# A fused attention and two-stage expert kernel: the first 256 tokens go through attention by themselves, and the first two tiles of the first layer are computed for each half of the first block

## The chip, the core and the metric

The kernel runs on one core of a Trainium2 chip. A core has a matrix engine (TensorE, PE in the rows; its weight loads are PEld), a vector engine (VectorE, DVE), a scalar engine (ScalarE, ACT), a general engine (GpSimd, POOL) and a queue engine (SyncE, SP), from which most transfers are issued. Each engine works through its own list of instructions in order and waits for the others by semaphores. The metric is the device time of one execution in microseconds (us), the median of several runs.

## What is computed

The reference has three stages, one behind the other, over 3072 tokens of width 512:

```python
for t in range(S):                                   # attention with a decaying state, 4 batches x 8 heads, S = 768
    state = gamma * state + outer(k[t], v[t])
    y[t] = scale * q[t] @ state
x = y.transpose(0, 2, 1, 3).reshape(3072, 512)
x = ((x @ w_a) * (x @ w_b)) @ w_out                  # first layer, d_ff 1536
e = argmax(x @ w_gate)                               # second layer: one of 8 experts for each token
out = gate * sigmoid_of_e * (relu(x @ w1[e]) @ w2[e])
```

The first layer's weights come as 64-bit numbers, and the kernel narrows them to pairs of 32-bit numbers (a high and a low part) on the chip.

## The kernel before

**Blocks.** The tokens are cut into seven blocks (BLOCKS, five of 512 tokens and two of 256). For each block the first layer runs over 12 tiles of 128 of its 1536 columns, counted by f. Tile f has two projections (`proj`, one bank p0 for w_a and one p1 for w_b, each 12 matmuls of 512 columns: 4 pieces of the model width, 3 matmuls each for high and low parts), then `act_a` (ScalarE copies p0 to a_sb), `gate` (VectorE multiplies p1 by a_sb into g_sb, L540; ScalarE casts g_sb to the high part of gs, L542; VectorE subtracts for the low part, L543), and one tile later `down` (12 matmuls that add gs times w_out into the banks acc0 to acc3). The banks p0 and p1 exist once: the second projection of tile f+1 can't start before the multiplication of tile f has read p1.

**Attention.** It goes by batches, two for every 256 tokens (one for each half of the heads). Batch n has `prep_q` and `prep_v` (decayed copies qd and vd, on VectorE or GpSimd), `scores` (matmuls L181 and L185 into two sc banks, VectorE masks them into m, L189, and adds up the states, L192; GpSimd decays the last state, L195) and `outputs` (matmuls L205 and L211 into two y banks, ScalarE copies, L217, VectorE adds, L220). For block 0 the result goes through a tile z straight into xs (high part by ScalarE, L223, low part by VectorE, L224); for the others it goes to xraw. While block j is in the first layer, the attention of block j+1 is run in slots between its projections (`attention_steps`, `steps`).

**Narrowing.** The weights arrive as 36 tiles of 512 KB, in the order of their use: w_a and w_b of f = 0, w_out of 0, w_a and w_b of 1, and then for each f the two projections of f + 2 and w_out of f + 1. Four buffers (wide) hold them raw. For each tile ScalarE makes e_cv (L441) and r_cv (L446), VectorE joins them in two operations on whole 128x512 tiles (L487, L489) into w_cv, ScalarE casts w_cv into the high part (L457), and GpSimd subtracts for the low part (L458); that lands in arena (w_a, w_b) or wos (w_out). The list of these steps is a generator, and `narrow(k)` takes the next k steps of it, four for each tile, two of them ending at one VectorE operation each. So the place of the narrow calls in the program fixes where these operations stand in each engine's list. In the first layer of block 0 there are 12 steps, three tiles, for each f: narrow(4) behind the first projection, behind the gate and behind down.

**The start.** `keep_warm` runs matmuls whose result isn't used. Then come the four attention batches of block 0 (batches 0 and 1 are the first 256 tokens, 2 and 3 the second), as steps of scores and outputs: scores 0, scores 1, outputs 0, scores 2, outputs 1, scores 3, outputs 2, outputs 3, with narrow(3) behind each from the third on. Only then does the first projection start, on all 512 tokens of block 0.

Of the kernel before, what the change touches and what calls it, by code (L numbers as in the profile page):

```python
# [7 lines left out]
F32 = mybir.dt.float32  # L8
# [35 lines left out]

NARROW_FROM, CONST_AT = 2, 5

# [7 lines left out]
def attention_moe_moe2(ctx: ExitStack, tc: tile.TileContext, a: dict, out: bass.AP):  # L54
# [54 lines left out]
    def f32(ap):  # L109
        return ap.bitcast(F32)  # L110
# [86 lines left out]
    def outputs(n, xr, toff):  # L197
# [14 lines left out]
        if xr is None:  # L212
            z, cols = p2.tile([128, 2, 256], F32, tag="gs", name="z"), slice(0, 256)
        else:
            z, cols = xr[:, 2 * pp : 2 * pp + 2], slice(toff, toff + 256)
# [12 lines left out]
    def prep_all(n):  # L228
        prep_q(n)
        prep_v(n)  # L230

    def attention_steps(j):
        own = [(ci, 2 * c + pp) for ci, c in enumerate(BLOCKS[j]) for pp in range(2)]

        def put(ci, n):
            if j == 0:
                xraw[j] = None
            elif j not in xraw:
                xraw[j] = p1.tile([128, KD, 512], F32, tag="xraw", name="xraw")
            outputs(n, xraw[j], 256 * ci)  # L240

        def s_a(n):
            scores(n)
            m = {0: 3, 1: 4, 2: None}.get(n, n + 2)
            if m and m < len(batches):
                load_batch(m)

        def s_b(ci, n, nxt):
            put(ci, n)
            if nxt is not None:  # L250
                prep_all(nxt)

        steps = []
        if j == 0:

            for i, (ci, n) in enumerate(own):
                steps.append(lambda n=n: s_a(n))
                if i:
                    steps.append(lambda p=own[i - 1], nxt=n + 1: s_b(*p, nxt if nxt <= len(own) else None))
            steps.append(lambda: s_b(*own[-1], None))  # L260
        else:
            for i, (ci, n) in enumerate(own):

                nxt = n + 1 if n + 1 < len(batches) and not (j == 1 and i + 1 == len(own)) else None
                steps.append(lambda n=n: s_a(n))
                steps.append(lambda ci=ci, n=n, nxt=nxt: s_b(ci, n, nxt))
        return steps
# [234 lines left out]
    def narrow(k):  # L502
        for _ in range(k):
            next(narrowing, None)
# [18 lines left out]

    def proj(j, f, ab, n):
        p = ps1.tile([128, 512], F32, tag=f"p{ab}", name=f"p{ab}")
        for k in range(KD):
            kk = slice(128 * k, 128 * k + 128)
            mm3(p[:, :n], arena[:, f, ab, 0, kk], arena[:, f, ab, 1, kk], xs[:, 0, k, :n], xs[:, 1, k, :n], k == 0, k == KD - 1)
        return p
# [7 lines left out]

    def gate(j, f, ta, pb, n):
        g = p1.tile([128, 512], F32, tag="g_sb", name="g_sb")
        dve.tensor_tensor(g[:, :n], pb[:, :n], ta[:, :n], op=ALU.mult)  # L540
        gs = p2.tile([128, 2, 512], F32R, tag="gs", name="gs")
        act.copy(gs[:, 0, :n], g[:, :n])  # L542
        dve.tensor_tensor(gs[:, 1, :n], g[:, :n], f32(gs[:, 0, :n]), op=ALU.subtract)  # L543
        gt[j, f] = gs

    accs = {}

    def down(j, f, ntile):
        gs, w = gt.pop((j, f)), wos.pop((j, f))
        for t in range(ntile):  # L550
# [226 lines left out]
    with tc.manual_schedule():  # L777
# [16 lines left out]
        load_batch(1)  # L794
        next_wide()
        load_batch(2)
        next_wide()
        next_wide()
        next_wide()
        tri_f = p1.tile([128, 2, 128], F32, tag="g_sb", name="tri_f")  # L800

        prep_all(0)
        prep_all(1)
        for n, st in enumerate(attention_steps(0)):
            st()
            keep_warm(WARM_STEP)
            if n >= NARROW_FROM:
                narrow(3)
            if n == CONST_AT:
                sync.dma_start(tri_f, a["tri"])  # L810
                sync.dma_start(base8, a["base8"])
                sync.dma_start(ident, a["ident"])
                sync.dma_start(wg, a["wg"])
                sync.dma_start(iota8, a["iota8"])
                sync.dma_start(pay, a["pay"])
                sync.dma_start(tab_d[:, :], a["tab0"])
        dve.tensor_copy(tri, tri_f)
        dve.tensor_copy(ohsum, base8)
        spare.clear()

        tok0 = 0
        route = []
        for j, blk in enumerate(BLOCKS):
# [4 lines left out]
            if last:  # L828
# [3 lines left out]
                route += [lambda: turn((0, 0), xs, LEAD), lambda: turn((0, 1), xs, LEAD + 128)]  # L832
            nslots = 3 * NF1 - 3
            lines = [att, route]
# [18 lines left out]

            for f in range(NF1):
                if f + 2 < NF1:
# [25 lines left out]
                if f > 0:  # L881
                    down(j, f - 1, ntile)
                if j == 0:
# [3 lines left out]
                if f == NF1 - 1:  # L887
                    down(j, f, ntile)
                slot()
# [115 lines left out]
```

## Time and profile before

| what | value |
|---|---|
| median of 3 runs | 1039.01 us (1038.29 to 1041.26) |
| the profiled execution, its own time | 1041.96 us |
| its span from first to last instruction | 1040.1 us |
| mean granted TensorE clock | 0.986 |
| first projection of block 0 starts | 37.27 us |
| first projection of block 1 starts | 155.95 us |

Between these two starts lies the first layer of block 0, with the narrowing of all weights and the attention of block 1. The profiled execution took 2.95 us more than the median of the runs, and 1.86 us of its own time lie outside its span. Places in the text are microseconds from the span's start.

### The profile page before, as it was taken

What the parts mean: (1) busy time and instruction counts of PE and PEld (TensorE: products, weight loads), DVE (VectorE), ACT (ScalarE), POOL (GpSimd) and SP (SyncE); (2) the same over time, 40 slices, a digit from 0 to 9 for tenths busy, and PEclk for the clock granted to TensorE, in tenths of its full rate; (3) what the DMA queues carried; (4) which work ended last, traced back from release to release, by engine and by line L of the source; (5) the groups of instructions that cost most, each with busy time, mean ns of one, the idle gap of its engine ahead of it and who ended that gap; (6) DMA issues with size and microseconds to landing.
All of it is one profiled execution on the core that took longest, in us unless ns stands there. A gap on an engine that the chain in (4) does not pass through costs nothing. (4 is left out here: it accounts for less than half of the span.)

```text
span 1040.1 us, 19789 instructions
## 1 busy us (share of the span) xinstructions
PE 1008.6 (97%) x7701; PEld 845.2 (81%) x7702; DVE 610.4 (59%) x1383; ACT 383.9 (37%) x775; POOL 278.9 (27%) x241
## 2 busy tenths in 40 slices
PE   6899999999999999999999999999999999999997
PEld 4687778887888788878888888999898978789996
DVE  5799886755577547755775484463365544345531
ACT  2466662222322332223222323553354434344431
POOL 1455541114111411132212333341322020221211
PEclk7799999999999999999999999999999999999999
DMA  8676635322433242234122422450564442435510
GB/s 326 205 236 215 224 122 176 129 82 53 154 110 101 84 153 98 85 94 159 55 91 62 127 88 71 132 183 21 182 203 156 157 155 102 155 134 167 190 67 28
DMA packets 51676, 138.63 MB, mean 133 GB/s; under 512 B 10973, under 2 KB 11229, under 8 KB 51552
## 3 DMA queue, kind: packets, MB, share of 16 engines
q1 hardware_dynamic: 43920, 117.16, 33.8%
q0 software_dynamic: 6928, 19.46, 5.9%
q8 instruction: 69, 1.13, 0.4%
q10 hardware_dynamic: 720, 0.57, 0.2%
q14 instruction: 39, 0.32, 0.1%
HBM read 121.37 MB, written 16.96 MB: 133 GB/s over the span
## 5 line engine op out<-in xcount | busy, mean ns | idle before, releaser
L105 PE MATMUL p<-xs,arena 128*128 128x512 f32 (+1 forms) x672 | 248.4, 370 | 8.7 <-DVE g_sb L540 4.5
L107 PE MATMUL p<-xs,arena 128*128 128x512 f32 (+1 forms) x672 | 242.4, 361 | 0.5 <-POOL arena L458 0.5
L106 PE MATMUL p<-xs,arena 128*128 128x512 f32 (+1 forms) x672 | 242.6, 361 | 0.0
L515 POOL TENSOR_TENSOR wos<-wo,wos 128x512 fp32r<-128x512 f32 x72 | 99.1, 1377 | 283.4 <-ACT wos L514 280.6
L105 PEld LDWEIGHTS p<-xs,arena 128*128 128x128 f32 x672 | 127.2, 189 | 32.4 <-issue 9.5
L107 PEld LDWEIGHTS p<-xs,arena 128*128 128x128 f32 x672 | 127.4, 190 | 20.7 <-POOL arena L458 1.0
L106 PEld LDWEIGHTS p<-xs,arena 128*128 128x128 f32 x672 | 127.4, 190 | 18.8
L542 ACT CAST gs<-g_sb 128x512 fp32r<-128x512 f32 (+1 forms) x84 | 47.0, 559 | 214.4 <-DVE g_sb L540 212.9
L340 DVE SCALAR_TENSOR_TENSOR junkd<-x,wcol 128x512 bf16<-128x512 f32 x144 | 121.1, 841 | 5.2 <-DMA wcol<-in_wgt 1.6
L105 PE MATMUL acc<-wos,gs 128*128 128x512 f32 x288 | 115.2, 400 | 0.0
L107 PE MATMUL acc<-wos,gs 128*128 128x512 f32 x288 | 113.2, 393 | 0.0
L106 PE MATMUL acc<-wos,gs 128*128 128x512 f32 x288 | 112.7, 391 | 0.0
L637 DVE SCALAR_TENSOR_TENSOR hs<-ph,hs 128x384 fp32r<-128x384 f32 (+2 forms) x72 | 40.1, 558 | 121.9 <-ACT hs L636 108.9
L671 DVE TENSOR_TENSOR arena<-wraw,arena 128x512 fp32r<-128x512 f32 x112 | 76.5, 692 | 48.4 <-ACT arena L670 38.6
L540 DVE TENSOR_TENSOR g_sb<-p,a_sb 128x512 f32<-128x512 f32 (+1 forms) x84 | 51.3, 611 | 79.2 <-PE p L107 70.1
L657 POOL DMA_INDIRECT out<-y,idx x27 | 27.9, 1032 | 237.2 <-ACT y L656 155.5
L105 PE MATMUL acc<-arena,hs 128*128 128x512 f32 x216 | 86.7, 402 | 2.1 <-ACT hs L636 1.5
L670 ACT CAST arena<-wraw 128x512 fp32r<-128x512 f32 x112 | 67.9, 616 | 49.7 <-PE acc L107 35.6
L107 PE MATMUL acc<-arena,hs 128*128 128x512 f32 x216 | 85.8, 397 | 0.0
L106 PE MATMUL acc<-arena,hs 128*128 128x512 f32 x216 | 85.4, 395 | 0.0
L636 ACT ACTIVATE hs<-ph 128x384 fp32r<-128x384 f32 (+2 forms) x72 | 35.4, 491 | 134.4 <-PE ph L107 88.9
L543 DVE TENSOR_TENSOR gs<-g_sb,gs 128x512 fp32r<-128x512 f32 (+1 forms) x84 | 52.3, 623 | 52.5 <-ACT gs L542 51.2
(147 smaller groups left out, 1698.8 us busy)
## 6 DMA issues: line engine op xcount, KB each, us to landing
wraw<-in_ex SPq DMA_DIRECT2D x64, 512.0 KB
wo<-wo_d SPq DMA_DIRECT2D x72, 256.0 KB
wide<-in_w_ab SPq DMA_DIRECT2D x24, 512.0 KB
qk<-in_qk SPq DMA_DIRECT2D x23, 512.0 KB
vk<-in_vk SPq DMA_DIRECT2D x23, 512.0 KB
wcol<-in_wgt SPq DMA_DIRECT2D x20, 512.0 KB
wide<-in_w_out SPq DMA_DIRECT2D x12, 512.0 KB
x_d<-x SPq DMA_DIRECT2D x24, 256.0 KB
```

Source lines behind the costliest of these rows:

```text
L105: pe.matmul(outp, lhsT=wh, rhs=rh, start=start, stop=False)
L106: pe.matmul(outp, lhsT=wh, rhs=rl, start=False, stop=False)
L107: pe.matmul(outp, lhsT=wl, rhs=rh, start=False, stop=stop)
L340: dve.scalar_tensor_tensor(junk, x2t[i], 1.0, wc[:, e], op0=ALU.mult, op1=ALU.mult, accum_out=st["lg"][:, e0 + e : e0 + e + 1])
L515: pool.tensor_tensor(w[:, 1], t, f32(w[:, 0]), op=ALU.subtract)
L540: dve.tensor_tensor(g[:, :n], pb[:, :n], ta[:, :n], op=ALU.mult)
L542: act.copy(gs[:, 0, :n], g[:, :n])
L543: dve.tensor_tensor(gs[:, 1, :n], g[:, :n], f32(gs[:, 0, :n]), op=ALU.subtract)
L636: act.activation(h[:, 0, :n], p[:, :n], AF.Relu)
L637: dve.scalar_tensor_tensor(h[:, 1, :n], p[:, :n], 0.0, f32(h[:, 0, :n]), op0=ALU.max, op1=ALU.subtract)
L670: act.copy(arena[:, f, part, 0], t[:, part])
L671: dve.tensor_tensor(arena[:, f, part, 1], t[:, part], f32(arena[:, f, part, 0]), op=ALU.subtract)
```

## The change

The 256 tokens of batches 0 and 1 are scored and finished first: scores 0, scores 1, outputs 0, outputs 1, with narrow steps between. Then comes scores 2, and then the first two tiles (f = 0 and 1, HALVES = 2) are computed on columns 0 to 255 of block 0 (`chunk(f, 0, ...)`), while scores 3, outputs 2 and outputs 3 stand between their projections; then `down` for the first two token tiles, and the same two tiles on columns 256 to 511. The loop over f starts at 2 for block 0, and the attention of block 1 starts there too: its 8 steps are spread over the 10 tiles that are left. A chunk is one half of a tile's two projections, with narrow(4) behind each; there are 16 narrow steps before the first chunk and 54 before f = 2. Before the change there were 18 before f = 0 and 42 before f = 2. The tile z takes its buffers from the ring of w_cv, the constant tri_f from that of wo, and the transfers of the constants move to the end of this part. The second layer and all later blocks are the same.

```diff
-NARROW_FROM, CONST_AT = 2, 5
+HALVES = 2
...
         if xr is None:
-            z, cols = p2.tile([128, 2, 256], F32, tag="gs", name="z"), slice(0, 256)
+            z, cols = e5.tile([128, 512], F32, tag="w_cv", name="z").rearrange("p (k n) -> p k n", k=2), slice(0, 256)
...
-    def proj(j, f, ab, n):
+    def proj(j, f, ab, n, c0=0):
...
-            mm3(p[:, :n], arena[:, f, ab, 0, kk], arena[:, f, ab, 1, kk], xs[:, 0, k, :n], xs[:, 1, k, :n], k == 0, k == KD - 1)
+            mm3(p[:, :n], arena[:, f, ab, 0, kk], arena[:, f, ab, 1, kk], xs[:, 0, k, c0 : c0 + n], xs[:, 1, k, c0 : c0 + n], k == 0, k == KD - 1)
...
-        for n, st in enumerate(attention_steps(0)):
-            st()
-            keep_warm(WARM_STEP)
-            if n >= NARROW_FROM:
-                narrow(3)
...
+        scores(0)
+        load_batch(3)
+        keep_warm(WARM_STEP)
+        narrow(2)
+        scores(1)
+        keep_warm(WARM_STEP)
+        narrow(4)
+        outputs(0, None, 0)
+        prep_all(2)
+        keep_warm(WARM_STEP)
+        outputs(1, None, 0)
+        prep_all(3)
+        narrow(6)
+        keep_warm(WARM_STEP)
+
+        spare[:] = ["acc2", "acc3"]
+        scores(2)
+        narrow(4)
+        rest = [lambda: (scores(3), load_batch(4)), lambda: (outputs(2, None, 256), prep_all(4)), lambda: outputs(3, None, 256), lambda: spare.clear()]
+
+        def chunk(f, c0, beside):
+            pa = proj(0, f, 0, 256, c0)
+            ta = act_a(pa, 256)
+            beside()
+            narrow(4)
+            pb = proj(0, f, 1, 256, c0)
+            gate(0, f, ta, pb, 256, c0)
+            beside()
+            narrow(4)
...
+        for f in range(HALVES):
+            chunk(f, 0, beside)
...
+        down(0, 0, 0, 2)
+        narrow(2)
+        for f in range(HALVES):
+            chunk(f, 256, lambda: None)
+            if f + 1 < HALVES or HALVES == 1:
+                down(0, f, 2 if f == 0 else 0, 4)
+            narrow(2)
...
-            nslots = 3 * NF1 - 3
+            f0 = 0 if j else HALVES
+            nslots = 3 * (NF1 - f0) - 3
...
-            for f in range(NF1):
+            for f in range(f0, NF1):
```

TensorE, ahead of the first projection (p_618 and p_452 are its bank p0, sc and y the banks of scores and outputs). Before, behind the outputs of batch 3:

```order
L205 MATMUL y<-qd,state 64x64 x16
L211 MATMUL y<-m,vd 64x64 x16
L783 LDWEIGHTS tri
L783 MATMUL wp<-tri 128x256
L105 MATMUL p_618<-xs,arena 128x512
L106 MATMUL p_618<-xs,arena 128x512
L107 MATMUL p_618<-xs,arena 128x512
```

Now, behind the scores of batch 2:

```order
L181 MATMUL sc<-qd,stage 64x64 x8
L185 MATMUL sc<-vd,stage 64x64 x8
L105 MATMUL p_452<-xs,arena 128x256
L106 MATMUL p_452<-xs,arena 128x256
L107 MATMUL p_452<-xs,arena 128x256
```

The first projection moved ahead of scores 3, outputs 2 and outputs 3, and it has half the columns.

VectorE, from the gate of tile 0 to that of tile 1. Before (g_sb_698 is tile 0, g_sb_807 tile 1):

```order
L540 TENSOR_TENSOR g_sb_698<-p1_685,a_sb_631 128x512
L543 TENSOR_TENSOR gs_700<-g_sb_698,gs_700 128x512
L489 SCALAR_TENSOR_TENSOR w_cv_642<-wide_430,w_cv_642 128x512
L487 SCALAR_TENSOR_TENSOR w_cv_712<-e_cv_640,r_cv_706 128x512
L489 SCALAR_TENSOR_TENSOR w_cv_712<-wide_492,w_cv_712 128x512
L487 SCALAR_TENSOR_TENSOR w_cv_723<-e_cv_710,r_cv_717 128x512
L489 SCALAR_TENSOR_TENSOR w_cv_723<-wide_559,w_cv_723 128x512
L487 SCALAR_TENSOR_TENSOR w_cv_749<-e_cv_721,r_cv_743 128x512
L220 TENSOR_TENSOR xraw_751<-xraw_751,y_752 128x2x2x64
L220 TENSOR_TENSOR xraw_751<-xraw_751,y_753 128x2x2x64
L540 TENSOR_TENSOR g_sb_807<-p1_794,a_sb_738 128x512
```

Now, for the second halves (g_sb_750 is tile 0, g_sb_821 tile 1):

```order
L529 TENSOR_TENSOR g_sb_750<-p1_737,a_sb_722 128x256
L534 TENSOR_TENSOR gs_540<-g_sb_750,gs_540 128x256
L478 SCALAR_TENSOR_TENSOR w_cv_735<-wide_593,w_cv_735 128x512
L476 SCALAR_TENSOR_TENSOR w_cv_763<-e_cv_733,r_cv_757 128x512
L478 SCALAR_TENSOR_TENSOR w_cv_763<-wide_660,w_cv_763 128x512
L476 SCALAR_TENSOR_TENSOR w_cv_797<-e_cv_761,r_cv_776 128x512
L478 SCALAR_TENSOR_TENSOR w_cv_797<-wide_689,w_cv_797 128x512
L529 TENSOR_TENSOR g_sb_821<-p1_808,a_sb_793 128x256
```

Almost as many joining operations (L476, L478, which were L487, L489) now stand between two gates of half a tile as stood between two of a whole one. In VectorE's whole list 17 of the 72 stood ahead of the last gate shown before, and 24 stand ahead of the last one shown now. Five more stand between that and the gate of tile 2, and six between two gates from there on, as before; so ahead of the gate of tile 9 there are 71 now, which is the number that stood ahead of the gate of tile 10.

GpSimd, around the preparation of batch 4 (qd_546 and vd_548 before, qd_584 and vd_586 now; the low part of w_b of tile 1, which is the fifth weight tile, is made from w_cv_614 before and from w_cv_516 now). Before:

```order
L458 TENSOR_TENSOR arena_84<-w_cv_378,arena_84 128x512
L139 TENSOR_TENSOR qd_546<-qk_259,dec_88 128x512
L146 TENSOR_TENSOR vd_548<-vk_260,vtab_89 128x512
L458 TENSOR_TENSOR wos_609<-w_cv_438,wos_609 128x512
L458 TENSOR_TENSOR arena_84<-w_cv_556,arena_84 128x512
L458 TENSOR_TENSOR arena_84<-w_cv_614,arena_84 128x512
```

Now:

```order
L195 TENSOR_TENSOR state_86<-state_86,gc_90 128x128
L447 TENSOR_TENSOR arena_84<-w_cv_441,arena_84 128x512
L139 TENSOR_TENSOR qd_584<-qk_510,dec_88 128x512
L146 TENSOR_TENSOR vd_586<-vk_511,vtab_89 128x512
L447 TENSOR_TENSOR arena_84<-w_cv_516,arena_84 128x512
```

The low parts of the third and fourth weight tile now stand ahead of batch 4, and that of the fifth stands right behind it. On SP the two transfers of batch 4 now stand behind the refills of all four wide buffers; before, they stood ahead of the first refill.

## Rows read from the trace of the kernel before

**Rows 1.** The page: busy time by engine, and TensorE's clock in 40 slices.

```profile
PE 1008.6 (97%) x7701; PEld 845.2 (81%) x7702; DVE 610.4 (59%) x1383; ACT 383.9 (37%) x775; POOL 278.9 (27%) x241
PEclk7799999999999999999999999999999999999999
```

**Rows 2.** Timeline of TensorE: start, duration, instruction, [idle before <- what ended it].

```profile
32.66 0.50 PE L783 MATMUL wp<-tri 128*128 128x256 bf16 x3
37.27 0.77 PE L105 MATMUL p<-xs,arena 128*128 128x512 f32 x1 [4.11 <-DVE z L220]
...
42.41 0.46 PE L181 MATMUL sc<-qd,qk 64*64 64x64 f32 x16
...
43.50 0.50 PE L105 MATMUL p<-xs,arena 128*128 128x512 f32 x1
...
49.20 0.69 PE L205 MATMUL y<-qd,state 64*64 64x64 f32 x32
...
50.30 0.50 PE L105 MATMUL p<-xs,arena 128*128 128x512 f32 x1
```

**Rows 3.** Waits of TensorE from 37 to 156 us: total, times, longest.

```profile
PE p L105 <- DVE z L220: 4.1, 1, 4.1
PE p L105 <- DVE g_sb L540: 3.3, 4, 1.2
PE y L205 <- DVE state L192: 1.1, 1, 1.1
PE p L107 <- POOL arena L458: 0.5, 1, 0.5
```

**Rows 4.** Windows from gate to gate, tiles 1 to 10: length, busy time (instructions).

```profile
57.38:66.47 9.09, 9.09 (x91) 7.34 (x91) 8.31 (x9) 6.34 (x11) 6.19 (x5) 1.00 0.61 188
...
sum 88.98, PE 85.02 PEld 67.83 DVE 80.44 ACT 57.74 POOL 48.53; mean PE 9.45 PEld 7.54 DVE 8.94 ACT 6.42 POOL 5.39
```

**Rows 5.** VectorE's groups in the same stretch: count | busy, mean ns | idle before.

```profile
L487 DVE SCALAR_TENSOR_TENSOR w_cv<-e_cv,r_cv 128x512 int32<-128x512 int32 x27 | 39.2, 1452 | 1.6 <-POOL arena L458 1.5
L489 DVE SCALAR_TENSOR_TENSOR w_cv<-wide,w_cv 128x512 int32<-128x512 int32 x27 | 25.6, 948 | 0.5
L543 DVE TENSOR_TENSOR gs<-g_sb,gs 128x512 fp32r<-128x512 f32 x9 | 6.4, 706 | 6.2 <-ACT gs L542 6.2
```

**Rows 6.** Waits of VectorE from 11 to 57.38 us: total, times, longest.

```profile
DVE w_cv L487 <- POOL arena L458: 4.5, 1, 4.5
DVE xs L224 <- ACT xs L223: 3.0, 4, 0.7
DVE z L220 <- ACT z L217: 1.9, 2, 1.1
...
DVE m L189 <- PE sc L185: 0.3, 1, 0.3
```

**Rows 7.** Timeline of VectorE around the gates of tiles 0, 1 and 10.

```profile
45.60 0.69 DVE L487 SCALAR_TENSOR_TENSOR w_cv<-e_cv,r_cv 128x512 int32<-128x512 int32 x1 [4.46 <-POOL arena L458]
46.21 0.75 DVE L189 TENSOR_TENSOR m<-sc,mask 128x256 f32<-128x256 f32 x2
...
47.71 0.68 DVE L540 TENSOR_TENSOR g_sb<-p,a_sb 128x512 f32<-128x512 f32 x1
...
54.40 0.69 DVE L489 SCALAR_TENSOR_TENSOR w_cv<-wide,w_cv 128x512 int32<-128x512 int32 x1
55.01 1.79 DVE L487 SCALAR_TENSOR_TENSOR w_cv<-e_cv,r_cv 128x512 int32<-128x512 int32 x1
...
146.36 0.68 DVE L540 TENSOR_TENSOR g_sb<-p,a_sb 128x512 f32<-128x512 f32 x1
```

**Rows 8.** Timeline of GpSimd: two low parts of weights.

```profile
26.23 1.31 POOL L458 TENSOR_TENSOR arena<-w_cv,arena 128x512 fp32r<-128x512 f32 x1 [1.98 <-ACT arena L457]
...
54.50 1.75 POOL L458 TENSOR_TENSOR arena<-w_cv,arena 128x512 fp32r<-128x512 f32 x1 [1.28 <-ACT arena L457]
```

**Rows 9.** Timeline of TensorE at the end of block 0.

```profile
138.16 0.47 PE L105 MATMUL p<-xs,arena 128*128 128x512 f32 x1 [0.99 <-DVE g_sb L540]
138.47 0.40 PE L106 MATMUL p<-xs,arena 128*128 128x512 f32 x1
138.70 0.40 PE L107 MATMUL p<-xs,arena 128*128 128x512 f32 x1
...
146.37 0.39 PE L107 MATMUL p<-xs,arena 128*128 128x512 f32 x1
147.19 0.47 PE L105 MATMUL p<-xs,arena 128*128 128x512 f32 x1 [0.43 <-DVE g_sb L540]
...
155.95 0.40 PE L105 MATMUL p<-xs,arena 128*128 128x512 f32 x1
```

**Rows 10.** Timeline of TensorE in a block of 256 tokens.

```profile
659.77 0.28 PE L106 MATMUL p<-xs,arena 128*128 128x256 f32 x1
659.89 0.28 PE L107 MATMUL p<-xs,arena 128*128 128x256 f32 x1
```

More of the change, by code (lines that the diff above doesn't have):

```diff
@@ L235, in put @@
         def put(ci, n):
-            if j == 0:
-                xraw[j] = None
-            elif j not in xraw:
+            if j not in xraw:
                 xraw[j] = p1.tile([128, KD, 512], F32, tag="xraw", name="xraw")
@@ L243, in s_a @@
             scores(n)
-            m = {0: 3, 1: 4, 2: None}.get(n, n + 2)
-            if m and m < len(batches):
-                load_batch(m)
+            if n + 2 < len(batches):
+                load_batch(n + 2)
         def s_b(ci, n, nxt):
@@ L253, in attention_steps @@
         steps = []
[L254 to L266, printed above, removed]
+        for i, (ci, n) in enumerate(own):
+            nxt = n + 1 if n + 1 < len(batches) and not (j == 1 and i + 1 == len(own)) else None
+            steps.append(lambda n=n: s_a(n))
+            steps.append(lambda ci=ci, n=n, nxt=nxt: s_b(ci, n, nxt))
         return steps
@@ L536, in act_a, with gate, down @@
         return t
-    def gate(j, f, ta, pb, n):
+    def gate(j, f, ta, pb, n, c0=0):
         g = p1.tile([128, 512], F32, tag="g_sb", name="g_sb")
         dve.tensor_tensor(g[:, :n], pb[:, :n], ta[:, :n], op=ALU.mult)
[L541 to L544, printed above, removed]
+        if (j, f) not in gt:
+            gt[j, f] = p2.tile([128, 2, 512], F32R, tag="gs", name="gs")
+        hi, lo = (gt[j, f][:, w, c0 : c0 + n] for w in range(2))
+        act.copy(hi, g[:, :n])
+        dve.tensor_tensor(lo, g[:, :n], f32(hi), op=ALU.subtract)
     accs = {}
-    def down(j, f, ntile):
-        gs, w = gt.pop((j, f)), wos.pop((j, f))
-        for t in range(ntile):
+    def down(j, f, t0, t1):
+        gs, w = gt[j, f], wos[j, f]
+        for t in range(t0, t1):
             if f == 0:
@@ L795, in attention_moe_moe2 @@
         next_wide()
+        next_wide()
         load_batch(2)
@@ L798, in attention_moe_moe2 @@
         next_wide()
-        next_wide()
-        tri_f = p1.tile([128, 2, 128], F32, tag="g_sb", name="tri_f")
+        tri_f = p2.tile([128, 512], F32, tag="wo", name="tri_f")[:, :256].rearrange("p (a n) -> p a n", a=2)
         prep_all(0)
         prep_all(1)
-        for n, st in enumerate(attention_steps(0)):
-            st()
-            keep_warm(WARM_STEP)
-            if n >= NARROW_FROM:
-                narrow(3)
[L809 to L816, printed above, removed]
+        scores(0)
@@ new lines, in chunk, with beside @@
+        def chunk(f, c0, beside):
[7 more added lines that the diff above has]
+            narrow(4)
+        def beside():
+            if rest:
+                spare[:] = ["acc2", "acc3"] if len(rest) == 3 else []
+                rest.pop(0)()
+        for f in range(HALVES):
+            chunk(f, 0, beside)
+        sync.dma_start(tri_f, a["tri"])
@@ new lines, in attention_moe_moe2 @@
+        sync.dma_start(base8, a["base8"])
+        down(0, 0, 0, 2)
[5 more added lines that the diff above has]
+            narrow(2)
+        sync.dma_start(ident, a["ident"])
+        sync.dma_start(wg, a["wg"])
+        sync.dma_start(iota8, a["iota8"])
+        sync.dma_start(pay, a["pay"])
+        load_batch(5)
+        sync.dma_start(tab_d[:, :], a["tab0"])
@@ L817, in attention_moe_moe2 @@
         dve.tensor_copy(tri, tri_f)
         dve.tensor_copy(ohsum, base8)
-        spare.clear()
         tok0 = 0
@@ L881, in attention_moe_moe2 @@
                 if f > 0:
-                    down(j, f - 1, ntile)
+                    down(j, f - 1, 0, ntile)
                 if j == 0:
@@ L887, in attention_moe_moe2 @@
                 if f == NF1 - 1:
-                    down(j, f, ntile)
+                    down(j, f, 0, ntile)
                 slot()
```

## The prediction, made before the changed kernel was run

> **What bounds the kernel now.** I read the page first. TensorE is busy for 97% of the span and its clock is below full only in the first slices, up to about 50 us [rows 1]. So after the start the end of the kernel moves with the end of TensorE's work, and the question is when the first layer of block 0 ends, that is when the first projection of block 1 starts: 155.95 us [rows 9]. All that follows is the same program as before. The timeline of TensorE then shows the start: the first projection begins at 37.27 us, behind a wait of 4.11 us [rows 2]. That looks like some ten microseconds that a change could give back to the matrix engine.
>
> The third view says who may keep them. From the start to block 1 TensorE's waits sum to only 9 us, and behind the first the longest sum, 3.3 us, is for VectorE's g_sb [rows 3]: the gate comes late and the bank p1 isn't free. The windows from the gate of tile 1 to the gate of tile 10 show VectorE busy for 80.44 of 88.98 us [rows 4]. What is missing is 6.2 us of waiting for ScalarE's half of the gate and 1.5 us for GpSimd [rows 5]; these 7.7 us and small gaps are all. VectorE never waits for TensorE in these 89 us. A gate stands in its list behind whole-tile joining operations, and it is done when they are done. So in block 0 from tile 1 on VectorE's list is the clock, and TensorE, with 85.02 busy of 88.98 us in modelled rows, follows it by a small margin that is used up at tiles 7 to 11. At the end of the list the roles change: the gate of tile 10 starts at 146.36 us [rows 7], the last projection that waits for it at 147.19 us, and from there TensorE runs at its own pace to 155.95 us [rows 9].
>
> Part of VectorE's load is blocking. A joining operation takes 0.69 us alone, and 1.79 us where GpSimd makes a low part beside it: that at 55.01 us ends behind the GpSimd operation of 54.50 us, which took 1.75 us [rows 7, 8]. The 54 in the windows took 39.2 + 25.6 = 64.8 us [rows 5], so 54 x 0.69 = 37.3 us of work and 27.5 us of blocking.
>
> The Trainium skill, in SBUF — State Buffer, section "SBUF: two separate sides", says that GpSimd and a VectorE operation with two inputs in SBUF hold one port pair by an exclusive lock, the loser waiting for the whole instruction. The rows bear it out. At its hardest, each low part of 1.31 us would fall fully on the two operations of its tile, 0.66 us each instead of the 27.5 / 54 = 0.51 us above; for the 24 operations that now stand ahead of the last half gate that is 24 x 0.15 = 3.6 us, and the time below would be 1045.0 instead of 1041.4 us.
>
> **The change as a sum on VectorE's list.** The amount of narrowing is the same, 72 joining operations; attention is the same. What changes is which tile's gate stands behind them. 71 of them stood ahead of the gate of tile 10 and now stand ahead of the gate of tile 9, because 54 instead of 42 narrow steps are taken ahead of tile 2. So I take the moment of that place in the list, 146.36 us, and correct it.
>
> Gates: ahead of it stood 10 whole gates, now 4 half pairs and 7 whole ones (tiles 2 to 8). A whole pair is 0.68 + 0.71 = 1.39 us [rows 5, 7]; for a half I take what a 128x256 operation took, two in 0.75 us [rows 7], so 0.75 a pair. 10 x 1.39 = 13.9 against 3.0 + 9.7 = 12.7: 1.2 us less. The wait inside a gate is 6.2 / 9 = 0.69 us [rows 5]; for a half I estimate 0.45, between half and all of it: 6.9 against 1.8 + 4.8 = 6.6, 0.3 us less.
>
> Early idle time: from 11 to 57.38 us VectorE waits 4.5 us for a low part, 4 x 0.7 = 3.0 us for ScalarE's part of xs, 1.9 us for z and 0.3 us for scores [rows 6], 9.7 us. The 4.5 us stood while TensorE ran its first, slow projection and the next weight steps were queued behind its copy; with the narrowing begun earlier this goes. The 3.0 us stay, since the order of copy, add, cast and subtract is the same. For z I keep 1.0 us: ScalarE now has its third e_cv step, which waits for a later weight tile, ahead of the first copy of z. And I keep 1.0 us for the low part of the fifth weight tile, which now stands behind batch 4 on GpSimd. So 5.0 us stay and 4.7 us go; the bounds are none and 6.7 us (all but the 3.0).
>
> The gate of tile 9 thus starts at 146.36 - 1.2 - 0.3 - 4.7 = 140.2 us. Behind the gate that stands at this place TensorE needed 155.95 - 146.36 = 9.6 us. But now one more tile is left: down, projection and projection, 36 matmuls. From 138.16 us to the end of the row of 146.37 us, one step of 0.23 us further, such a tile without a wait took 8.4 us [rows 9]. 140.2 + 9.6 + 8.4 = 158.2 us against 155.95: **2.3 us later**. With the profiled execution's own time that is 1044.3 us; that execution stood 2.95 us above the median of the runs, so against the median 1039.0 + 2.4, rounded, it is **1041.4 us**.
>
> The rest costs nothing where it stands. Matmuls of 256 columns start 0.12 us apart [rows 10], those of 512 columns 0.23 us [rows 9]; the four half chunks are 96 of the first instead of 48 of the second, 11.5 against 11.0 us. TensorE waits for VectorE there, and that hides it; without this cover it is 0.5 us. Moving attention of block 1 behind tile 2 moves one batch, a scores and an outputs step of 43.50 - 42.41 = 50.30 - 49.20 = 1.1 us each [rows 2], into a stretch in which TensorE waits anyway; on VectorE it was counted, since all four batches are done by tile 9 as they were by tile 10. The constants that SP now sends later are first used in block 1. That z takes a buffer of w_cv makes z of batch 2 wait for the low part of the fourth weight tile, which is needed by the projection beside it in any case; if it held VectorE, 1.31 us [rows 8].
>
> A rule speaks against half tiles: the Trainium skill, Perfetto Trace Analysis, section "Matmuls", says that larger matmuls are more efficient than smaller ones. The trace agrees, at the price of the 0.5 us above; if TensorE paid it the time would be 1041.9 us.
>
> **The rivals.** *TensorE keeps its lead.* The first projection could start when the first low part is there, at 26.23 + 1.31 = 27.5 us [rows 8], 9.7 us earlier than 37.27. Scores 3 and two outputs then lie behind it, 3 x 1.1 us, and 0.5 us is lost on half tiles: 5.9 us earlier, 1033.1 us. For it speak the wait of 4.11 us and the low clock at the start [rows 1, 2]. Against it: VectorE's gate of tile 9 would have to start by 155.95 - 5.9 - 18.0 = 132.0 us, 8.2 us before my sum, so nearly a third of the 27.5 us of blocking would have to vanish. It decides if the joining operations fall more often beside GpSimd's idle time.
>
> *GpSimd's line holds TensorE and VectorE.* Batch 4 is now loaded behind four refills, and the low part of the fifth weight tile stands behind its preparation. If the batch lands late, all three engines stop, as VectorE did for 4.46 us at 45.60 us [rows 7]. Then none of the 4.5 us of early idle time goes: 1041.4 + 4.5 = 1045.9 us. It decides once that low part is ready later than the second projection of tile 1 is due.
>
> *The change moves nothing.* If all 6.7 us of early idle time go, the sum is 155.95 + 0.3 us, and the earlier start and the longer tail cancel: 1039.3 us.
>
> **How the numbers follow.** I give my sum 0.55, TensorE's lead 0.22, the held GpSimd line 0.13, and nothing moved 0.10. The sum's own range is 1037.5 to 1046.0 us: no idle time saved gives 1041.4 + 4.7 = 1046.1, and all of it together with a fifteenth of the blocking less (1.8 us) gives 1037.5. To hold 8 in 10 the range must reach most of the way to TensorE's lead: 1033.5 to 1046.5 us, with a tenth left out on either side. A measurement of this kernel tells about 0.3%, 3.1 us, from no change: below 1035.9 us lies nearly all of the first rival, 0.20; above 1042.1 us the second one and two fifths of my own case, 0.35; between them 0.45.
>
> **What would show it.** In the changed profile the first projection should start at 25 to 28 us; the 24th joining operation should still stand ahead of the second half's gate of tile 1, with no VectorE wait for TensorE in tiles 2 to 9; TensorE's wait for g_sb should grow beyond 3.3 us; the gate of tile 9 should start near 140 us and the first projection of block 1 near 158 us. From there to the end both profiles should take the same time. I am wrong if the first projection of block 1 starts before 153 us, most likely because the joining operations take less than 1.2 us each (64.8 / 54), or because VectorE stood less in the first 45 us than I keep; and wrong the other way if GpSimd is seen waiting for in_qk or in_vk around 35 us while TensorE waits for arena.

## The result and the profile after

The changed kernel is slower: 1049.6 us in the median of 4 runs (1047.5 to 1052.2) against 1039.16 us of the kernel before, ratio 1.0093 with a 95% interval of 1.0079 to 1.0108. The forecast was 1041.4 us, with a range up to 1046.5. The profiled execution took 1052.2 us, its span is 1050.5 us.

The page, busy time and granted clock, which answers to [rows 1]:

```profile
PE 1011.7 (96%) x7737; PEld 851.3 (81%) x7738; DVE 608.5 (58%) x1387; ACT 385.0 (37%) x779; POOL 278.8 (27%) x241
PEclk8799999999999999999999998999999999999999
```

TensorE has nearly the same work (1011.7 against 1008.6 us busy), and its share of the span has fallen by one point. TensorE's timeline shows the start that answers to [rows 2], the waits in the half tiles, and the end of the first layer of block 0, which answers to [rows 9]:

```profile
25.53 0.58 PE L105 MATMUL p<-xs,arena 128*128 128x256 f32 x1 [1.14 <-ACT arena L446]
...
36.37 0.39 PE L107 MATMUL p<-xs,arena 128*128 128x256 f32 x1 [2.19 <-POOL arena L447]
...
43.74 0.39 PE L107 MATMUL p<-xs,arena 128*128 128x256 f32 x1 [2.75 <-POOL arena L447]
...
53.93 0.50 PE L105 MATMUL acc<-wos,gs 128*128 128x512 f32 x1 [2.93 <-ACT gs L533]
...
153.85 0.50 PE L105 MATMUL p<-xs,arena 128*128 128x512 f32 x1 [1.24 <-ACT a_sb L524]
...
164.95 0.39 PE L105 MATMUL p<-xs,arena 128*128 128x512 f32 x1
```

The first projection starts 11.7 us earlier than before, and the first projection of block 1 comes 9.0 us later, 164.95 against 155.95 us. Behind it the two executions are nearly alike: 1050.5 - 164.95 = 885.5 us against 884.1. So 9.0 us of the loss lie in block 0.

VectorE's timeline, gates of tiles 2, 3, 9 and 10, with the two waits that stand ahead of tile 3's, answers to [rows 7]:

```profile
69.30 0.68 DVE L529 TENSOR_TENSOR g_sb<-p,a_sb 128x512 f32<-128x512 f32 x1
...
79.27 1.77 DVE L476 SCALAR_TENSOR_TENSOR w_cv<-e_cv,r_cv 128x512 int32<-128x512 int32 x1 [2.58 <-POOL arena L447]
82.47 0.75 DVE L220 TENSOR_TENSOR xraw<-xraw,y 128x256 f32<-128x256 f32 x2 [1.43 <-ACT xraw L217]
83.14 0.68 DVE L529 TENSOR_TENSOR g_sb<-p,a_sb 128x512 f32<-128x512 f32 x1
...
146.09 0.68 DVE L529 TENSOR_TENSOR g_sb<-p,a_sb 128x512 f32<-128x512 f32 x1
...
153.83 0.69 DVE L529 TENSOR_TENSOR g_sb<-p,a_sb 128x512 f32<-128x512 f32 x1 [3.97 <-ACT a_sb L524]
```

The gate of tile 9, behind 71 joining operations, starts at 146.09 us. That is where the gate of tile 10 stood before, behind the same 71, at 146.36 us. VectorE has won nothing on its list, and one more tile is left behind it: 164.95 - 146.09 = 18.9 us. From tile 2 to tile 3 it needs 13.84 us.

The groups of VectorE from 11 us to that place (busy, mean ns, idle before) show its joining operations, and its gates, whole and half, which answer to [rows 5]:

```profile
L478 DVE SCALAR_TENSOR_TENSOR w_cv<-wide,w_cv 128x512 int32<-128x512 int32 x35 | 39.1, 1118 | 0.8
L476 DVE SCALAR_TENSOR_TENSOR w_cv<-e_cv,r_cv 128x512 int32<-128x512 int32 x36 | 37.9, 1053 | 7.6 <-POOL arena L447 6.4 <-DMA wo_d<-w_cv 1.1
...
L534 DVE TENSOR_TENSOR gs<-g_sb,gs 128x512 fp32r<-128x512 f32 x7 | 4.9, 699 | 4.8 <-ACT gs L533 4.8
L529 DVE TENSOR_TENSOR g_sb<-p,a_sb 128x512 f32<-128x512 f32 x7 | 4.8, 681 | 0.0
...
L534 DVE TENSOR_TENSOR gs<-g_sb,gs 128x256 fp32r<-128x256 f32 x4 | 2.8, 706 | 1.9 <-ACT gs L533 1.9
L529 DVE TENSOR_TENSOR g_sb<-p,a_sb 128x256 f32<-128x256 f32 x4 | 1.7, 414 | 0.0
```

The same stretch of the kernel before, two groups and the windows whose two parts make it up (length, busy):

```profile
L487 DVE SCALAR_TENSOR_TENSOR w_cv<-e_cv,r_cv 128x512 int32<-128x512 int32 x36 | 49.5, 1375 | 6.1 <-POOL arena L458 6.0
L489 DVE SCALAR_TENSOR_TENSOR w_cv<-wide,w_cv 128x512 int32<-128x512 int32 x35 | 33.2, 950 | 0.7
...
sum 135.36, DVE 115.76; mean DVE 57.88
```

The windows of the changed kernel:

```profile
sum 135.09, DVE 112.62; mean DVE 56.31
```

VectorE stood still for 135.36 - 115.76 = 19.6 us before and for 135.09 - 112.62 = 22.5 us now. The same 71 joining operations took 82.7 us before and take 77.0 us now.

### The profile page after: what moved, and what is told of

Read it like the earlier page. It is cut to its first block, busy times and chain, and to the rows that moved or that the text cites. A ratio compares the mean times of both kernels' runs of the same rounds, so it can differ in the third digit from the quotient of the medians.

```text
span 1050.5 us, 19877 instructions
## 1 busy us (share of the span) xinstructions
PE 1011.7 (96%) x7737; PEld 851.3 (81%) x7738; DVE 608.5 (58%) x1387; ACT 385.0 (37%) x779; POOL 278.8 (27%) x241
## 5 line engine op out<-in xcount | busy, mean ns | idle before, releaser
L105 PE MATMUL p<-xs,arena 128*128 128x512 f32 (+1 forms) x688 | 252.6, 367 | 4.1 <-ACT arena L446 1.4
L107 PE MATMUL p<-xs,arena 128*128 128x512 f32 (+1 forms) x688 | 246.3, 358 | 5.5 <-POOL arena L447 5.5
L106 PE MATMUL p<-xs,arena 128*128 128x512 f32 (+1 forms) x688 | 246.1, 358 | 0.0
L105 PEld LDWEIGHTS p<-xs,arena 128*128 128x128 f32 x688 | 131.3, 191 | 26.8 <-DVE g_sb L529 2.2
L107 PEld LDWEIGHTS p<-xs,arena 128*128 128x128 f32 x688 | 131.4, 191 | 25.2 <-POOL arena L447 6.3
L106 PEld LDWEIGHTS p<-xs,arena 128*128 128x128 f32 x688 | 131.7, 191 | 18.1
```

Of the source, the lines that this page charges most:

```text
L105: pe.matmul(outp, lhsT=wh, rhs=rh, start=start, stop=False)
L106: pe.matmul(outp, lhsT=wh, rhs=rl, start=False, stop=False)
L107: pe.matmul(outp, lhsT=wl, rhs=rh, start=False, stop=stop)
```

## The experiments

Theory A: transfers eat what VectorE was to win. Batch 4 is loaded behind refills, and batch 5 now stands behind the half tiles, beside the constants and batch 6. Theory B: the tail, one more tile left to TensorE alone when the narrowing ends. Theory C: half tiles themselves are slow.

Each ratio below is to the kernel before on the same chip (its medians were 1041.18 to 1041.81 us there, 1039.16 for the row of the changed kernel). The times are places in us in one profiled execution: the gate of tile 2, VectorE's gate behind 71 joining operations, the first projection of block 1, and the tail, which is the last less the one before it. In the versions with half tiles the first projection of block 0 starts at 25.5 to 26.8 us. The two rows with one join of two are one execution each and have no ratio, since their weights are others.

| run | ratio (95%) | gate of 2 | list's place | block 1 | tail |
|---|---|---|---|---|---|
| before | 1 | 66.47 | 146.36 (tile 10) | 155.95 | 9.6 |
| changed | 1.0093 (1.0079 to 1.0108) | 69.30 | 146.09 (tile 9) | 164.95 | 18.9 |
| loads of 4 and 5 early | 1.0049 (1.0032 to 1.0067) | 66.35 | 140.55 (9) | 159.38 | 18.8 |
| 42 steps ahead | 1.0007 (0.9994 to 1.0021) | 63.54 | 145.19 (10) | 154.74 | 9.6 |
| both edits | 0.9992 (0.9979 to 1.0005) | 62.65 | 144.35 (10) | 153.92 | 9.6 |
| before, 54 steps ahead | 1.0044 (1.0026 to 1.0061) | 70.24 | 141.65 (9) | 160.48 | 18.8 |
| batch 4 early | 1.0090 (1.0071 to 1.0109) | 68.53 | 145.44 (9) | 164.24 | 18.8 |
| batch 5 earlier | 1.0059 (1.0041 to 1.0077) | 67.95 | 141.55 (9) | 160.35 | 18.8 |
| constants later | 1.0075 (1.0058 to 1.0092) | 70.61 | 146.06 (9) | 164.91 | 18.9 |
| early loads, 54, 10 a tile | 0.9991 (0.9978 to 1.0004) | 67.53 | | 153.45 | |
| early loads, 48, 11 a tile | 0.9998 (0.9988 to 1.0007) | 65.48 | | 153.96 | |
| before, 54, 10 a tile | 0.9977 (0.9967 to 0.9988) | 69.79 | | 154.75 | |
| changed, one join of two | | 60.27 | | 150.18 | |
| before, one join of two | | 59.30 | | 146.42 | |
| both edits, 50 + 16 fillers | 1.0021 (1.0006 to 1.0036) | 67.37 | 148.41 (10) | 157.98 | 9.6 |
| 48 and 11, 50 + 16 fillers | 1.0001 (0.9989 to 1.0013) | 67.95 | | 156.43 | |
| both edits, 50 fillers | 0.9984 (0.9975 to 0.9992) | 62.60 | 144.12 (10) | 153.71 | 9.6 |
| 48 and 11, 50 fillers | 0.9977 (0.9965 to 0.9990) | 65.86 | | 154.33 | |

**Loads, steps, and both.** The edits of the loads:

```diff
         scores(1)
+        load_batch(4)
...
-        rest = [lambda: (scores(3), load_batch(4)), lambda: (outputs(2, None, 256), prep_all(4)), lambda: outputs(3, None, 256), lambda: spare.clear()]
+        rest = [lambda: (scores(3), load_batch(5)), lambda: (outputs(2, None, 256), prep_all(4)), lambda: outputs(3, None, 256), lambda: spare.clear()]
...
-        load_batch(5)
```

> The changed kernel, with batch 4 loaded right behind scores 1 (not behind scores 3) and batch 5 behind scores 3 (not behind the half tiles). Theory A, transfers (late batches, a cluster of loads at 65 to 80 us, eat the idle time that was to be saved, 5 to 7 us on VectorE): 1043 to 1045 us, the gate of tile 9 at 139 to 141 us instead of 146.1, no wait of GpSimd for batch 4 near 36 us. Theory B, only the longer tail costs: 1049.6 us within 1.5. Theory C, half tiles themselves hold VectorE back: 1049.6 us too.

Those of the steps, 42 instead of 54 ahead of tile 2 (`narrow(k)` in `chunk`, with k = 4 for the first halves):

```diff
-            chunk(f, 256, lambda: None)
+            chunk(f, 256, lambda: None, 1)
```

> The changed kernel, with 42 instead of 54 narrow steps ahead of tile 2, as before the change; loads untouched. Theory B, tail (one more tile left to TensorE alone when the narrowing ends): the narrowing ends at tile 10 again, first projection of block 1 near 157 instead of 164.95 us, 1041 to 1042 us. Theory A, transfers alone: 1048 to 1050 us. Theory C, half tiles: 1048 to 1050 us.

> Both edits, of the loads and of the steps. If A and B both hold and add up: 1049.6 - 8.2 - 6 = 1035 us, faster than both kernels, first projection of block 1 near 151 us. If the two are one and the same loss: 1041 to 1042 us. Theory C: 1048 to 1050 us.

And 54 steps in the kernel before, with its whole tiles and its own loads:

```diff
             if n >= NARROW_FROM:
-                narrow(3)
+                narrow(5)
```

> The kernel before the change, with whole tiles and its own order of attention and loads, and five instead of three narrow steps behind each of six attention steps, so 54 ahead of tile 2. Theory B, tail: VectorE's list comes to the gate of tile 9 at 146.36 - 1.39 - 0.69 = 144.3 us and 18.0 us of TensorE follow, first projection of block 1 at 162.3 instead of 155.95 us, 1045.5 us (up to 1047.5 if no time is won). Theories A and C: no change, 1038 to 1040.5 us.

Both A and B are borne out, each in its own place: the loads move the list's place from 146.09 to 140.55 us and leave the tail, the steps shorten the tail from 18.9 to 9.6 us. The kernel before with 54 steps shows that the tail needs no half tile. Theory C isn't borne out: half tiles with 42 steps give a ratio of 1.0007, and with 54 steps whole tiles (1.0044) and half tiles with early loads (1.0049) come out alike. The rows of the kernel before with 54 steps, VectorE's gate of tile 9 and the first projection of block 1:

```profile
141.65 0.68 DVE L540 TENSOR_TENSOR g_sb<-p,a_sb 128x512 f32<-128x512 f32 x1
...
160.48 0.39 PE L105 MATMUL p<-xs,arena 128*128 128x512 f32 x1
```

The tail is the same in all six runs with 54 steps ahead and 12 a tile, 18.8 to 18.9 us. Expected was 162.3 for 160.48 us; the list came to its place sooner than foreseen, at 141.65 for 144.3 us. What failed is the sum: both edits together are 0.8 us better than the steps alone in block 0, not 6. With 42 steps the weights are wanted later, and late loads cost little: ScalarE waits 0.7 us for refills from 60 to 90 us, where it is 5.6 us in the changed kernel. Nor was the result faster than before.

**Which load.** Each edit of the loads alone, and the constants (ident, wg, iota8, pay, tab_d) sent at tile 5 with batch 5 left in its place:

> The changed kernel with only batch 4 loaded behind scores 1, all else as changed. If GpSimd's line held by batch 4 is the main loss by transfers: gate of tile 9 at 141 to 142 instead of 146.1 us, ratio 1.005 to 1.006. If the cluster of loads behind the half tiles is the main loss: gate of tile 9 at 145 to 146 us, ratio 1.008 to 1.010.

> The changed kernel with only batch 5 loaded earlier, directly behind batch 4 and scores 3. If the cluster of loads is the main loss: gate of tile 9 at 141 to 142 us, ratio 1.005 to 1.006. If GpSimd's line is: 145 to 146 us, 1.008 to 1.010.

> The changed kernel with the transfers of ident, wg, iota8, pay and tab_d moved from behind the half tiles to tile 5, batch 5 left in its late place. If these constants are what crowds the weight refills at 65 to 80 us: gate of tile 9 at 142 to 143 instead of 146.1 us, ratio 1.005 to 1.007. If it is batch 5, 1 MB beside batch 6 and the refills: 145 to 146 us, ratio 1.008 to 1.010.

Of the two batches it is batch 5. With batch 4 early GpSimd no longer waits for it, TensorE's wait of 2.75 us at 43.74 us becomes one of 1.04 us, and the time stays. With batch 5 earlier both of these waits are there (3.33 and 2.69 us), and the place falls to 141.55 us. Here are SyncE's issues in the changed kernel at 65 to 73 us:

```profile
67.54 0.36 SPq L130 DMA_DIRECT2D qk<-in_qk  x1
68.00 0.38 SPq L131 DMA_DIRECT2D vk<-in_vk  x1
68.43 0.65 SPq L845 DMA_DIRECT2D tab_d<-in_tab  x1
69.19 0.51 SPq L422 DMA_DIRECT2D wide<-in_w_ab  x1
69.80 0.37 SPq L130 DMA_DIRECT2D qk<-in_qk  x1
70.27 0.65 SPq L131 DMA_DIRECT2D vk<-in_vk  x1
72.02 0.33 SPq L422 DMA_DIRECT2D wide<-in_w_ab  x1
```

Batches 5 and 6, four transfers of 512 KB, go out within 2.7 us around a refill, just when the narrowing wants one. In the windows from 70 to 80 us the DMA share (the last column but one) is full:

```profile
70.00:75.00 5.00, 5.00 (x82) 3.98 (x81) 4.30 (x4) 3.37 (x6) 2.67 (x2) 1.00 0.99 384
75.00:80.00 5.00, 5.00 (x23) 4.09 (x22) 2.38 (x4) 2.21 (x4) 2.05 (x2) 1.00 1.03 373
```

ScalarE's wait for refills from 60 to 90 us (total, times, longest):

```profile
ACT e_cv L430 <- DMA wide<-in_w_ab: 5.6, 2, 3.4
```

The time of the refills of the tile wide from issue to landing, 55 to 90 us:

```profile
DMA to landing us min/median/max: 3.2/4.9/9.1
```

The same two views with batch 5 earlier, the wait first:

```profile
ACT e_cv L430 <- DMA wide<-in_w_ab: 1.5, 2, 1.1
```

And the landing:

```profile
DMA to landing us min/median/max: 3.3/4.9/5.2
```

The refill issued at 72.02 us, behind both batches, took 9.1 us to land, where none took more than 5.2 with batch 5 earlier. ScalarE's first step on a weight tile waited for 5.6 us instead of 1.5, and behind it GpSimd's low part and VectorE. VectorE's step from the gate of tile 2 to that of tile 3 is 10.95 us with batch 5 earlier, 13.84 in the changed kernel. The Trainium skill, in DMA: Bandwidth & Descriptors, section "Queues, rings and completion order", says that each DMA engine takes the descriptors of a ring in their order; the refills stand behind the batches in SyncE's queue, and the trace agrees. The constants are not settled: the ratio lies between the two expectations, and the place, 146.06 us, is 1.3 us earlier only if counted from a first projection that started 1.3 us later.

**Where the early start went.** If the tail and the loads are put right, TensorE's start 11 us earlier is still not seen in the time. First, the narrowing spread evenly, 11 steps a tile instead of 12 (this edit in one place of the loop over f) or 10 (in two):

```diff
-                    narrow(4)
+                    narrow(3)
```

> The changed kernel with batches 4 and 5 loaded early, 54 narrow steps ahead of tile 2 as in the changed kernel, and from tile 2 on 10 narrow steps a tile instead of 12, so that the narrowing lasts until tile 11. Theory B, tail: the early start counts at last, since TensorE is left alone with no whole tile: first projection of block 1 at 149 to 151 us (159.38 with 12 steps a tile, 153.92 with 42 steps ahead), ratio to the kernel before 0.994 to 0.996. Theory D, the half tiles and the denser attention of block 1 keep the gain wherever the narrowing ends: 153 to 155 us, ratio 0.998 to 1.000.

> A version between the runs so far: batches 4 and 5 early, 48 narrow steps ahead of tile 2 and 11 a tile behind. If VectorE's list and TensorE's own pace are both just met: first projection of block 1 at 151 to 152.5 us, ratio 0.996 to 0.998. If the sum of VectorE's list alone sets the end, however it is spread: 153 to 154.5 us, ratio 0.998 to 1.000.

> The kernel before the change with 54 narrow steps ahead of tile 2 and 10 a tile from there. Theory B, tail: the loss of the run with 54 and 12 (ratio 1.0044, first projection of block 1 at 160.48 us) goes and turns into a gain, 151 to 154 us, ratio 0.995 to 0.998. Theory D: VectorE and TensorE have the same work and only the start counts, ratio 0.999 to 1.001, 155 to 157 us.

Neither version with half tiles can be told from the kernel before: both intervals hold 1. Now TensorE is the bound from tile 2 on: with 48 steps and 11 a tile it is busy for all of the 88.48 us from the gate of tile 2 to block 1, and VectorE waits for it at 7 of its 14 gates, six of them from tile 2 on (total, times, longest, from 11 to 155 us):

```profile
DVE g_sb L529 <- PE p L107: 7.0, 7, 3.7
```

The kernel before with 54 steps ahead and 10 a tile comes out at 0.9977, the best ratio without fillers and the one that theory B gave, though its first projection of block 1, 154.75 us, is only 1.2 us earlier and not at 151 to 154 us. Theory B's places with half tiles, 149 to 151 us, were not reached; 153.45 us and 0.9991 are what theory D gave. Next, VectorE's list was cut by half of its joining operations:

```diff
-                dve.scalar_tensor_tensor(wi, t[:, :, 1], -0x80000000, wi, op0=ALU.bitwise_and, op1=ALU.bitwise_or)
```

> The changed kernel without the second of the two joining operations of each weight tile (the sign bit is left out, so weights and routing are others, and only the time of block 0 is to be read). Theory: VectorE's list is the clock of block 0 and keeps the early start from counting. Then 36 operations of about 1.1 us less let TensorE run at its own pace, 12 tiles of 8.4 us with 14 attention steps of 1.1 us behind the start: first projection of block 1 at 141 to 146 us, with TensorE's earlier start kept, 5 to 8 us ahead of the kernel before with the same cut. Rival: transfers or the half tiles hold TensorE, 153 us or later, and not ahead of it.

> The kernel before the change without the second joining operation (sign bit left out; only block 0 is to be read). Theory: TensorE at its own pace from its start, first projection of block 1 at 147 to 151 us. Rival: transfers hold both kernels alike, 153 us or later.

The theory behind these fell. With the change TensorE comes to block 1 later, 150.18 against 146.42 us, not 5 to 8 us earlier. VectorE's timeline, the gate of tile 2 with the change:

```profile
60.27 0.68 DVE L528 TENSOR_TENSOR g_sb<-p,a_sb 128x512 f32<-128x512 f32 x1
```

Without it:

```profile
59.30 0.69 DVE L539 TENSOR_TENSOR g_sb<-p,a_sb 128x512 f32<-128x512 f32 x1 [0.35 <-PE p L107]
```

From the first projection at 25.53 and 35.71 us to there it is 34.7 us with half tiles and 23.6 us without. So the early start is spent ahead of tile 2. From tile 2's gate to block 1 it is 89.9 against 87.1 us; two more attention steps of block 1, of 1.1 us each, are left to TensorE there and would be 2.2 of the 2.8 us. Two things could spend it: the half clock, granted from 20 to about 33 us and around 46 us in the run with both edits, or the parts of the weights, which aren't there yet. Fillers raise the clock:

```diff
+        keep_warm(50)
         scores(2)
...
+            if f and not c0:
+                keep_warm(8)
             pa = proj(0, f, 0, 256, c0)
+            if f and not c0:
+                keep_warm(8)
             pb = proj(0, f, 1, 256, c0)
```

> The run with both edits (loads early, 42 narrow steps ahead of tile 2) with more of the fillers that the kernel has already: 50 ahead of scores 2 and 8 ahead of each first-half projection of tile 1. It tells what eats TensorE's early start ahead of tile 2. If the half clock (granted 0.5 from 20 to 33 us and from 45 to 47 us): the clock is 1.0 there, gate of tile 2 at 59 to 60.5 instead of 62.65 us, ratio 0.996 to 0.998. If the weights' parts and VectorE: TensorE's waits for arena grow by what the clock gives, gate of tile 2 at 62 to 63 us, ratio 0.999 to 1.000.

> The same fillers in the version with 48 narrow steps ahead of tile 2 and 11 a tile behind, where the profile shows TensorE as the bound from tile 2 on. If the clock eats the start: gate of tile 2 at 63 instead of 65.48 us and all of it kept, ratio 0.996 to 0.998. If weights and VectorE do: 65 us, ratio 0.999 to 1.000.

Both are spoilt: the 16 fillers of tile 1 write acc3, which attention has borrowed, and waited themselves for VectorE's sum (4.28 us at 38.24 us in the first). So the 50 ahead of scores 2 alone:

> The run with both edits and 50 fillers ahead of scores 2 alone; the 16 fillers of tile 1 are gone, which waited themselves for VectorE's sum z (4.3 and 5.4 us) since they share a bank with attention. If TensorE's half clock from 20 to 33 us eats its early start: gate of tile 2 at 60 to 61.5 instead of 62.65 us, ratio 0.996 to 0.998. If VectorE and the weights' parts do: the first half gate stays at 35 to 36 us, gate of tile 2 at 62 to 63 us, ratio 0.999 to 1.000.

> The same 50 fillers in the version with 48 narrow steps ahead of tile 2 and 11 a tile behind. Clock: gate of tile 2 at 63 to 64.5 instead of 65.48 us, ratio 0.997 to 0.999. VectorE and the weights' parts: 65 to 66 us, ratio 0.9995 to 1.0005.

With them, on both edits, the windows from 20 to 45 us (granted clock in the last column but two):

```profile
20.00:25.00 5.00, 4.56 (x95) 3.90 (x93) 3.42 (x5) 2.30 (x5) 1.27 (x1) 1.00 0.77 304
25.00:30.00 5.00, 3.41 (x78) 2.86 (x78) 4.93 (x9) 4.15 (x9) 2.98 (x2) 1.00 0.27 88
30.00:35.00 5.00, 3.12 (x77) 2.58 (x76) 4.76 (x13) 2.07 (x5) 3.48 (x5) 1.00 0.74 197
35.00:40.00 5.00, 3.43 (x46) 3.21 (x50) 3.29 (x7) 2.92 (x7) 3.93 (x3) 0.58 1.01 399
40.00:45.00 5.00, 4.72 (x54) 4.21 (x47) 3.29 (x7) 3.63 (x8) 1.52 (x2) 0.50 0.35 110
```

TensorE's wait in the first projection of tile 1:

```profile
36.57 0.58 PE L107 MATMUL p<-xs,arena 128*128 128x256 f32 x1 [2.84 <-POOL arena L447]
```

The windows without the fillers:

```profile
25.00:30.00 5.00, 3.27 (x16) 2.71 (x12) 4.82 (x7) 4.17 (x9) 2.46 (x2) 0.50 0.17 47
30.00:35.00 5.00, 5.00 (x125) 4.70 (x128) 4.76 (x14) 2.56 (x6) 3.50 (x4) 0.64 0.79 215
35.00:40.00 5.00, 3.43 (x108) 2.88 (x98) 3.25 (x8) 2.40 (x6) 4.47 (x4) 1.00 1.00 392
40.00:45.00 5.00, 2.98 (x15) 2.58 (x16) 3.77 (x8) 4.01 (x9) 1.50 (x2) 0.88 0.39 144
```

And the wait:

```profile
37.09 0.39 PE L107 MATMUL p<-xs,arena 128*128 128x256 f32 x1 [1.21 <-POOL arena L447]
```

At full clock TensorE is done sooner and waits for the low part, 2.84 instead of 1.21 us, and the gate of tile 2 is at 62.60 for 62.65 us. The half clock isn't gone, it has moved: from 35 to 45 us the granted clock is 0.58 and 0.50 with the fillers, 1.00 and 0.88 without. Even so the first two half gates come 9.6 and 19.4 us behind the first projection with them (25.71, 35.31 and 45.15 us) and 9.6 and 19.0 us without (26.24, 35.83 and 45.20 us). So the clock isn't what eats the early start. From 25 to 35 us VectorE, whose list holds the joining of the weights and attention, is busy for 9.7 of 10 us with the fillers and for 9.6 without: there its list is the pace, and the early start runs into it. From 35 to 45 us it is busy for 6.6 and 7.0 of 10 us only. Refills, low parts and z of the second 256 tokens follow one another there, and no run separates them.

Block 0 also ends where it did, 153.71 for 153.92 us. The ratios of the last two runs, 0.9984 and 0.9977, lie below those without fillers, 0.9992 and 0.9998, but the intervals overlap. In the profiled executions the difference lies behind block 0, in code that is the same (1036.4 - 153.71 = 882.7 us against 1040.2 - 153.92 = 886.3 us), and the twelve executions with both edits differ among themselves by up to 4.9 us. A gain by the fillers isn't shown.

## Why the prediction was wrong

**What held.** VectorE's list was the clock of block 0: from 11 us to the gate of tile 9 the changed kernel shows no wait of VectorE for TensorE. The first projection came at 25.53 us, foreseen at 25 to 28. The tail was the largest term and nearly right: 9.6 + 8.4 = 18.0 us foreseen, 18.9 measured; most of the rest is the wait of 1.24 us for a_sb at 153.85 us, where a wait of 0.43 us for g_sb stood before [rows 9].

**The step that failed** is "Early idle time": "So 5.0 us stay and 4.7 us go", taken for the whole change of VectorE's idle time. Up to the place in the list that idle time rose from 19.6 to 22.5 us. Without the waits inside the gates, 6.9 us before and 6.7 us now, that is 3.1 us more instead of 4.7 us less, 7.8 us off. The windows of VectorE in the changed kernel (length, busy) up to the second half gate of tile 1, and from there, show where:

```profile
11.00:60.10 49.10, 40.34 (x69) 0.76 0.61 215
60.10:146.09 85.99, 72.28 (x95) 1.00 0.69 228
```

The first window of the kernel before, up to the gate of tile 1:

```profile
11.00:57.38 46.38, 35.31 (x67) 0.74 0.69 249
```

In the first window idle time without the gates' waits fell from 10.4 to 7.4 us, 3.0 instead of 4.7 us. The wait of 4.5 us for a low part [rows 6] is 1.4 us now, but z takes 2.1 instead of the 1.0 us kept, and a wait for in_vk that the sum left out went from 1.2 to 1.8 us. In the second window (88.98 us, 80.44 busy before [rows 4]) the sum had no new idle time at all, and there it rose from 2.3 to 8.4 us, by 6.1 us: 4.9 instead of 1.5 us for low parts, 1.4 for attention of block 1, 1.1 for a transfer out of w_cv. So 1.7 of the 7.8 us are the early term, and 6.1 us a term that was put at nothing.

One reason is a load that the sum passed over: the prediction follows batch 4 and the constants past the refills, and never batch 5, which `load_batch` sends behind the half tiles, at 67.54 us instead of 43.44. Moved forward, it alone brings the place 4.5 us earlier. The same two windows of that run show that 3.3 us of idle time go behind the half tiles (13.7 to 10.5 us), while 0.9 us more stand ahead; the other 2.2 us are busy time.

```profile
11.00:59.20 48.20, 38.54 (x69) 0.75 0.70 242
59.20:141.55 82.35, 71.89 (x97) 1.00 0.69 227
```

What makes the rest of the new idle time, 2.8 us behind the half tiles, no run shows.

**Other terms were off too**, and nearly cancel. Gates were to cost 1.2 us less; they cost 14.2 instead of 13.8 us, since a half pair took 0.41 + 0.71 = 1.12 us on average, where 0.75 us was put down. The four low parts took 0.60, 0.42, 0.43 and 1.38 us, so most of this is one that ran long. The blocking of the 71 joining operations was held constant and fell by 5.7 us. What is left of VectorE's busy time rose by 2.2 us: 112.62 - 77.0 - 14.2 = 21.4 us against 115.76 - 82.7 - 13.8 = 19.3. (This is a remainder: instructions overlap in the rows, so it isn't the sum of the smaller groups.) Together 3.1 + 0.4 + 2.2 - 5.7 - 0.2 (gate waits) = -0.2 us, which is the place at 146.09 instead of 146.36 us. The foreseen place, 140.2 us, is met by the run with both loads early (140.55 us), but not for the foreseen reason: VectorE still stands for 129.55 - 108.12 = 21.4 us there, and the joining operations take 72.9 us.

From 158.2 to 164.95 us these make 6.75 us: 5.9 on the list, 0.9 in the tail. 1.4 us more lie behind block 0 in this pair of executions.

**The rivals.** GpSimd's line held by batch 4 was the sign of being wrong the other way, and it is in the trace, with TensorE's wait of 2.75 us beside it:

```profile
39.57 1.45 POOL L139 TENSOR_TENSOR qd<-qk,dec 128x512 f32<-128x512 f32 x1 [3.25 <-DMA qk<-in_qk]
```

It cost next to nothing: without it the ratio is 1.0090, and the place is 0.7 us earlier. That its price, 4.5 us, is also what batch 5 cost is luck. That TensorE keeps its lead was wrong for a reason that the prediction had not seen: most of the lead is spent ahead of tile 2, not by VectorE's load behind it. Up to 35 us VectorE's list spends it; what does so from there to tile 2 stays open. TensorE's wait for g_sb, which was to grow beyond 3.3 us, shrank to 0.8 us; waits for parts of the weights (6.9 us) and for gs (2.9 us) stand in its place.

## What to carry to other kernels

Where one engine's list is the clock, find the place at which it hands over to the next engine, and count what is left to that one alone: here 9.2 to 9.3 us more, whichever way the tiles were cut. List every transfer that a reordering moves, not only those it names; here one 1 MB batch that went out among the refills of a stream cost 4.5 us on the list, about what the prediction hoped to win there. Look for new idle time behind the part that is changed, too. An earlier start is worth something only if what feeds it can be earlier too.

## What the runs showed of the hardware

- The same 71 joining operations took 82.7, 77.0, 75.5 and 72.9 us of VectorE (before, changed, batch 5 earlier, both loads early), where 71 x 0.69 us would be 49.0. The Trainium skill, in SBUF — State Buffer, section "SBUF: two separate sides", says that whichever of a GpSimd operation and a VectorE operation with two inputs in SBUF starts first gets the shared port pair for its whole instruction. That the order and the times of the loads move the sum by 10 us fits it. Such a blocking can't be held constant when an order changes.
- A low part of half the columns, 128x256, took 0.71 us on average in the changed kernel (0.57 with batch 5 earlier), a whole one 0.70. But the average hides 0.42 us at 47.34 us and 1.38 us at 61.02 us: the half one is the shorter operation, and its average is set by the one that ran long.
- 50 small matmuls of 0.12 us put the granted clock at 1.00 from 25 to 35 us, where it was 0.50 and 0.64. After TensorE's wait of 2.84 us, which ended at 36.57 us, it was 0.58 and then 0.50 up to 45 us, where it was 1.00 and 0.88 without them.
